# The causal mask added by VectorE's evictions, and the first mixture's results turned as 128 tokens and a stacked rest

## The chip, the cores and the metric

The kernel runs on one core of a Trainium2 chip. Five engines work side by side: TensorE (PE in the profile; its weight loads have a row of their own, PEld), VectorE (DVE), ScalarE (ACT), GpSimd (POOL) and SyncE (SP), which issues most DMAs. The metric is the device time of one execution in microseconds. Three runs before the change gave 395.3, 395.41 and 395.61 us, median 395.41 us.

## The reference: what is computed

```
# attention: B=2, H=8, S=576, D=64
scores = q @ k^T / 8
cum    = cumsum(max(s, 0))
scores = where(key later than query, -1e9, scores + min(-(cum_q - cum_k), 0))
x      = softmax(scores) @ v                       -> 1152 tokens of 512 numbers
# first mixture: 8 experts, at most `capacity` tokens each
e      = argmax(x @ w_gate);   g = softmax(x @ w_gate)[e]
x      = g * (max(x @ w1[e], 0) @ w2[e])           (0 for tokens beyond the capacity)
# second mixture: 8 experts, no capacity, own weights and a bias per modality
e      = argmax(x @ w_gate + bias[modality]);  g = softmax(...)[e]
out    = g * (max(x @ w1[e], 0) @ w2[e])
```

## The kernel before the change

**Attention** (up to about 96 us) goes over 8 pairs of heads, 16 heads (`for n in range(17)`, from line 612). A head's 576 queries are five tiles (`ROWS`, `QS`): 64 and four times 128. Their scores stand in four PSUM banks (`BANKS`): tiles 2 and 1 in the first, 3 and 0 in the second, tile 4 in two halves. `scores` (L474) fills a bank by two products (`qa`,`ka` and `qb`,`kb`; the second carries the rest of the precision and the sums of s). Where a bank reaches the diagonal, a third matmul adds the mask: the identity in bf16 (`identb`) is the weights, and `later`, 0 or -8e9, is what goes through. Then VectorE evicts every tile of the bank in one instruction (L510): scores times -0.125 into `sc`, and their running minimum into `nmx`. ScalarE takes the exponential with its sum (L515). One head later TensorE turns the exponentials block by block (`turned`, `pt`), VectorE and ScalarE copy them to `eT`, and `values` multiplies by v (`pa`, `pb`) once a pair; `close_pair` turns the results to tokens (`px`). GpSimd prepares the operands of the next pair (L370, L371, L377). All matmuls of attention stand in the order in which `pe` (L426) writes them; the other engines' order is set by a scheduler.

**First mixture** (111 to 264 us): eight slots of up to 192 tokens, one per expert, 160, 192, 136, 152, 132, 160, 144 and 168 wide (`WID`). TensorE's order is written by hand (`pin`): `mul` issues the products of the slot, and `step` moves a clock on, by which the generator `tail1` of the slot before is resumed between them. `tail1` computes the second mixture's logits from `yT` (features by tokens), then `back(k, yr, 0)` and `back(k, yr, 1)` turn the results to tokens: first 96 tokens, then the rest, four matmuls against the identity each (`pty`, L993), one for each 128 features. ScalarE evicts them times the gate into `yr` (L994). One DMA (L1067) writes `yr`, 2 x 96 rows of 520 numbers (512 results, gate, token, logits' bias), to `y1` in DRAM. The second mixture gathers its tokens from `y1` (L830).

**Second mixture** (264 us to the end): five slots, of which `tail2` also uses `back`.

Weights come by SP as pieces of 512 KB (`fetch`, L144 and L146), 7 of 8 ahead, into 8 buffers; SP issues its DMAs in order and waits at each.

Of the kernel before, what the change touches and what calls it, by code (L numbers as in the profile page):

```python
# [23 lines left out]
H1, H2, W1, W2, C1, C2 = HC[1], HC[2], W[1], W[2], C[1], C[2]  # L24
# [3 lines left out]
RW2 = 520  # L28
GATE, TOK, BIAS = 512, 513, 520
# [8 lines left out]
NOV = 7  # L38
# [54 lines left out]
def build(tc, ctx, spots, tab, qk, v, s, wg, wa, cap, mod, wg2, mb, wb, out):  # L93
    nc = tc.nc
    P = 128
# [5 lines left out]
    y1 = dram.tile([NCH * C1, RW2], F32, name="y1")  # L101
# [7 lines left out]
    ident = const.tile([P, P], F32, name="ident")  # L109
    ctab = const.tile([P, tab.shape[1]], F32, name="ctab")  # L110
    con = {}
    for name, (c0, shape) in spots.items():
        if len(shape) == 1:
            con[name] = ctab[:, c0:c0 + shape[0]]
        else:
# [11 lines left out]
                                 op0=ALU.add, op1=ALU.add)  # L127
# [11 lines left out]
    def fetch(src, e, i, pin=False):  # L139

        st = wst.tile([P, PIECE], F32, name="st")
        c0 = i * PIECE
        if isinstance(e, int):
            ins = nc.sync.dma_start(st, src[e, :, c0:c0 + PIECE])  # L144
        else:
            ins = nc.sync.dma_start(st, src[bass.ds(e, 1), :, c0:c0 + PIECE].rearrange("o p c -> (o p) c"))  # L146
        if pin:
            tc.keep_in_program_order(ins)
        return st

    first, xcs, written = [], [], []

    def awake(ps, a, b, n):

# [72 lines left out]
    with ExitStack() as actx:  # L227
        ap = actx.enter_context(tc.tile_pool(name="ap", bufs=2))
        ae = actx.enter_context(tc.tile_pool(name="ae", bufs=1))
# [19 lines left out]
        with tc.issue_after(pads.ins):  # L249
            summed = summed()  # L250
        make_identity(nc, ident)
        identb = ae.tile([P, P], BF16, name="identb")
        nc.gpsimd.tensor_copy(identb, ident)
        later = ae.tile([P, P + 64], BF16, name="later")
        nc.gpsimd.memset(later, 0.0)
        for c0, c1 in ((0, P), (P, P + 64)):
            nc.gpsimd.affine_select(out=later[:, c0:c1], in_=later[:, c0:c1], pattern=[[-1, c1 - c0]],
                                    compare_op=ALU.is_ge, fill=-8.0e9, base=0, channel_multiplier=1)
        ebuf = {}
        for t in range(1, NT):  # L260
            for j in range(2):
# [162 lines left out]
        def pe(op, *args, **kw):  # L424
            with tc.issue_after(order[-1]) if order else ExitStack():
                ins = op(*args, **kw)  # L426
            order[:] = [ins.ins]
            return ins
# [7 lines left out]
        def open_pair(p):  # L436
            pr_ = Part()
            pr_.p, pr_.b, pr_.hp, pr_.eTs = p, p // 4, p % 4, []
            pr_.qa, pr_.ka, pr_.qb, pr_.kb, pr_.vt = loads.pop(p)
            pairs.append(pr_)  # L440
            if p < 7:
                loads[p + 1] = load(p + 1)
            if p > 3:
                for i in range(2):
                    first.append(fetch(wa, 0, 2 * (p - 4) + i, pin=True))
            if p == 3:
                for i in range(2):
                    xc = const.tile([H1, 2, RW], F32, name=f"xc{i}")
                    with tc.issue_after(operands[-1]):
                        nc.gpsimd.memset(xc, 0.0)  # L450
                    xcs.append(xc)
                zrow = ac.tile([P, 1, DM], F32, name="zrow")
                with tc.issue_after(operands[-1]):
                    nc.gpsimd.memset(zrow, 0.0)
                tc.keep_in_program_order(nc.sync.dma_start(
                    out.rearrange("(p t) d -> p t d", t=9), zrow.to_broadcast([P, 9, DM])))

# [16 lines left out]
        def scores(h, bank, parts=(0, 1)):  # L474


            k, i = h.k, h.i
            qa, ka, qb, kb = k.qa[:, i], k.ka[:, i], k.qb[:, i], k.kb[:, i]
            if 0 in parts:
                h.ps[bank] = pss.tile([P, 512], F32, name="ps")  # L480
            ps = h.ps[bank]
            for t, o0, c0, c1 in bank:
                r, q0 = ROWS[t], QS[t]
                o = ps[:r, o0:o0 + c1 - c0]
                if 0 in parts:
                    pe(nc.tensor.matmul, o, qa[:, q0:q0 + r], ka[:, c0:c1], start=not o0, stop=False,
                       skip_group_check=True)
                if 1 in parts:
                    pe(nc.tensor.matmul, o, qb[:, q0:q0 + r], kb[:, c0:c1], start=False, stop=c1 <= q0,
                       skip_group_check=True)  # L490
            if 1 not in parts:
                return
            del h.ps[bank]
            t, o0, c0, c1 = bank[0]
            if t == 2:
                masked = ps[:, P:512].rearrange("p (u c) -> p u c", u=2)[:, :, 64:192]
                mask = later[:, 0:P].unsqueeze(1).to_broadcast([P, 2, P])
            elif t == 3:
                masked, mask = ps[:, 320:512], later
            else:  # L500
                masked, mask = ps[:, QS[4] - c0:c1 - c0], later[:, 0:P]
            if c1 > QS[t]:
                pe(nc.tensor.matmul, masked, identb, mask, start=False, stop=True, skip_group_check=True)
            for t, o0, c0, c1 in bank[::-1]:
                r, w = ROWS[t], QS[t] + ROWS[t]
                if c0 == 0:
                    h.sc[t] = ap.tile([P, S], F32, name="sc", bufs=3)
                low = h.nmx[t][:r] if c0 else 3.0e38
                h.nmx[t] = ap.tile([P, 1], F32, name="nmx", bufs=6)
                least[:] = [nc.vector.tensor_scalar(h.sc[t][:r, c0:c1], ps[:r, o0:o0 + c1 - c0], -0.125, low, op0=ALU.mult,  # L510
                                                    op1=ALU.min, accum_out=h.nmx[t][:r]).ins]
                if c1 == w:
                    n = 2 * k.hp + i
                    to = ebuf[t, i][:, :w] if t else ebuf[1, i][0:64, P:P + 64]
                    recent[:] = [nc.scalar.activation(to, h.sc[t][:r, :w], AF.Exp, bias=h.nmx[t][:r],  # L515
                                                      scale=-1.0, accum_out=rsum[:r, k.b, t, n:n + 1]).ins]

        moved, least = [], []
# [93 lines left out]
        for n in range(2 * 2 * 4 + 1):  # L612
# [24 lines left out]
            if n == 1:  # L637
                fills = tc.issue_after(filled.ins)
                fills.__enter__()
                for bb in range(B):  # L640
# [10 lines left out]
                                        fill=0.0, base=0, channel_multiplier=-1)  # L651
# [183 lines left out]
    def pin(ins):  # L835

        tc.keep_in_program_order(ins)
# [151 lines left out]
    def back(k, yr, i):  # L989
        r0, r = k.rows[i]  # L990
        pt = pt_.tile([r, DM], F32, tag="t", name="pty")
        for dt in range(DM // P):
            pin(nc.tensor.transpose(pt[:, dt * P:(dt + 1) * P], k.yT[:, dt, r0:r0 + r], ident))  # L993
        nc.scalar.mul(yr[:r, i, 0:DM], pt, k.xc[:r, i, GATE:GATE + 1])  # L994

    def absent(k):
        inv = mp.tile([HP, W[k.m]], F32, tag="inv", name="inv")
        nc.vector.tensor_scalar(inv, k.idx, float(OFF[k.m]), NONE, op0=ALU.is_ge, op1=ALU.mult)
        return inv

    def tail1(k, c):

        k.yr, l8 = yrs[c % 2], l8s[c % 2]
        nc.gpsimd.tensor_copy(k.yr[:, :, TOK], k.xc[:, :, TOK])
        yield k.T[0]
        p8 = pq.tile([P, k.c], F32, tag="q", name="p8")
        for kt in range(4):
            pin(nc.tensor.matmul(p8[32 * kt:32 * kt + 32], wg2s[:, kt, :], k.yT[:, kt, :], start=True, stop=True,
                   tile_position=(0, 32 * kt)))
        nc.vector.tensor_copy(l8[:, 0:k.c], p8)  # L1010
        back(k, k.yr, 0)
        yield k.T[1]
        pl = pq.tile([H1, 2, P], F32, tag="q", name="pl")
        for i in range(2):
            pin(nc.tensor.transpose(pl[:, i, :], l8[:, i * H1:(i + 1) * H1], ident))
        yield k.T[2]
        back(k, k.yr, 1)
        bc = [H1, 2, E]
        lg = mp.tile(bc, F32, name="lg2")
        nc.vector.tensor_reduce(lg, pl.rearrange("p i (k e) -> p i e k", k=4)[:, :, 0:E, :], axis=AX.X, op=ALU.add)  # L1020
# [41 lines left out]
        g = mp.tile([H1, 2], F32, name="g2")  # L1062
        nc.vector.tensor_reduce(g, ex, axis=AX.X, op=ALU.add)
        nc.vector.tensor_scalar_add(g, g, 1.0e-9)
        nc.vector.reciprocal(k.yr[:, :, GATE], g)

        nc.sync.dma_start(y1[c * C1:(c + 1) * C1, :].rearrange("(i p) w -> p i w", i=2), k.yr)  # L1067
        yield k.T[6] if k.early else k.T[4]
        for i in range(2):
            pin(nc.tensor.matmul(pl2, pos[:, i, :], colm[:, i, :], start=(c == 0 and i == 0), stop=True,  # L1070
# [195 lines left out]
    def clear(x):  # L1266
        tc.keep_in_program_order(nc.gpsimd.memset(x, 0.0))

    yrs = [sm.tile([H1, W1, RW2], F32, name=f"yr{i}") for i in range(2)]
    l8s = [sm.tile([P, C1], F32, name=f"l8{i}") for i in range(2)]  # L1270
    at(0, 2, lambda: clear(xcs[2]))
    for lst in (lists, list2):
# [148 lines left out]
    with tc.If(more_ > 0):  # L1421
        latest.clear()
        nc.sync.dma_start(y1[E * C1:, :].rearrange("(p t) d -> p t d", p=H1),
                          yrs[0][:, 0:1, :].to_broadcast([H1, NOV * W1, RW2]))
        tot1 = nc.values_load(reso[0:1, 0, NOV:NOV + 1], min_val=0, max_val=NOV)
        with tc.If(tot1 > 0):
            latest.clear()
            again()
            beyond()
            nested(1, tot1, reso, list1b, 0, NOV, wa, lambda k, i: tail1(k, E + i))  # L1430
            listed(list2[:H2], pl2, 2)
            left()
            latest.clear()
        tot2 = nc.values_load(info["res"][0:1, 0, NSLOT2:NSLOT2 + 1], min_val=0, max_val=NSLOT2)
        nested(2, tot2, info["res"], list2, 0, NSLOT2, wb, lambda k, i: tail2(k))
        latest.clear()
# [47 lines left out]
```

## Time and profile before

| what | value |
|---|---|
| median of three runs | 395.41 us |
| the profiled execution | 396.09 us |
| its span in the profile | 394.0 us (2.1 us lie around it) |
| TensorE busy | 380.8 us, 97% of the span |
| VectorE, ScalarE, GpSimd busy | 196.7, 178.9, 130.0 us |
| granted TensorE clock, mean | 0.996 |
| chain that ended last, share of TensorE | 82% |

How to read it: busy times are averages over stages with different limits, so the stages are read one by one. Matmuls overlap, and a row's duration is longer than the step to the next row; what one costs in a row of matmuls is the difference of two starts. The chain of waits is followed back from the last instruction and shows which engine the end hung on at each time.

### The profile page before, as it was taken

To read this page: it belongs to the slowest core of one execution; us is meant where nothing else is said; L and a number is where in the kernel's file an instruction comes from. 1 tells how busy PE (TensorE), PEld (TensorE's weight loads), DVE (VectorE), ACT (ScalarE), POOL (GpSimd) and SP (SyncE) were. 2 spreads that over 40 slices of the span, in tenths; PEclk is the share of its full clock that TensorE was granted. 3 is DMA by queue.
4 is the path that set the end of the run, shared out by engine and by line. 5 is a ranking of instruction groups with operands and counts; after the bars stand their busy time and mean duration, and the time that the engine had idled before them with its cause. 6 is when DMAs were issued, how large, how long until landed. Compare 5 with 4: busy or idle time off the path is not lost.

```text
span 394.0 us, 8765 instructions
## 1 busy us (share of the span) xinstructions
PE 380.8 (97%) x3128; PEld 355.6 (90%) x3128; DVE 196.7 (50%) x785; ACT 178.9 (45%) x473; POOL 130.0 (33%) x180
## 2 busy tenths in 40 slices
PE   6799999999999999999999999999999999999993
PEld 3688888898689999999999999999999999999992
DVE  6977779987826773341515061559822335211110
ACT  6999999987315642121212121255423464131130
POOL 4776877660164221330202003000335256010020
PEclk9999999999999999999999999999999999999998
DMA  5865699802159962978798779871279356010010
GB/s 186 289 192 157 235 378 364 284 3 79 51 142 303 352 222 62 321 230 294 221 326 262 241 238 278 262 246 56 59 255 342 107 166 208 26 38 21 2 54 24
DMA packets 26882, 74.63 MB, mean 189 GB/s; under 512 B 5527, under 2 KB 7959, under 8 KB 26828
## 3 DMA queue, kind: packets, MB, share of 16 engines
q1 hardware_dynamic: 24120, 66.73, 50.6%
q0 software_dynamic: 2624, 7.19, 6.5%
q8 instruction: 27, 0.44, 0.5%
q14 instruction: 27, 0.22, 0.2%
q10 hardware_dynamic: 84, 0.04, 0.0%
HBM read 63.97 MB, written 10.62 MB: 189 GB/s over the span
## 4 chain that ended last, share of the span: by engine, by line
PE 82%; issue 7%; DMA 4%; DVE 3%; POOL 2%; POOLq 0%; SPq 0%; ACT 0%; DVEq 0%; ACTq 0%
PE ps L907 30%; PE ps L915 7%; PE ps L916 7%; PE ps L917 7%; PE ps L426 6%; PE pt L426 6%; PE pb L426 4%; PE ps L911 3%; PE pty L993 3%; PE pa L426 2%; PE ptx L871 2%; PE px L426 2%; DMA out<-yo,oi 2%; PE ps L913 1%; DMA qkd<-in_qk 1%
## 5 line engine op out<-in xcount | busy, mean ns | idle before, releaser
L907 PE MATMUL ps<-xn,st 128*128 128x160 f32 (+6 forms) x512 | 70.4, 290 | 0.3 <-ACT xn L892 0.3
L907 PEld LDWEIGHTS ps<-xn,st 128*128 128x128 f32 x512 | 66.2, 190 | 0.5 <-ACT xn L892 0.4
L907 PE MATMUL ps<-hidden,st 128*128 128x160 f32 (+5 forms) x448 | 62.4, 293 | 0.0
L907 PEld LDWEIGHTS ps<-hidden,st 128*128 128x128 f32 x448 | 58.5, 190 | 0.0
L515 ACT ACTIVATE e<-sc,nmx 128x192 f32<-128x192 f32 (+4 forms) x80 | 44.8, 561 | 2.2 <-DVE sc L510 2.1
L973 DVE COPY yT<-ps 128x276 f32<-128x276 f32 (+6 forms) x22 | 8.0, 362 | 69.6 <-ACT yT L972 69.6
L915 PE MATMUL ps<-xs,hi 128*128 128x276 f32 x128 | 38.5, 300 | 0.0
L915 PE MATMUL ps<-hidden,hi 128*128 128x276 f32 x128 | 38.1, 298 | 0.0
L917 PE MATMUL ps<-xs,lo 128*128 128x276 f32 x128 | 37.2, 290 | 0.0
L916 PE MATMUL ps<-xs,hi 128*128 128x276 f32 x128 | 37.1, 290 | 0.0
L917 PE MATMUL ps<-hidden,lo 128*128 128x276 f32 x128 | 37.1, 290 | 0.0
L916 PE MATMUL ps<-hidden,hi 128*128 128x276 f32 x128 | 37.1, 290 | 0.0
L830 POOL DMA_INDIRECT xc<-x,idx x14 | 14.9, 1064 | 60.1 <-DVE eq L1030 44.2
L972 ACT COPY yT<-ps 128x276 f32<-128x276 f32 (+6 forms) x22 | 7.1, 322 | 60.6 <-PE ps L907 33.2
L426 PE MATMUL pt<-ident,e 128*128 128x128 f32 x224 | 33.0, 275 | 0.8 <-ACT eT L537 0.7
L510 DVE TENSOR_SCALAR_CACHE_REDUCE sc<-ps 128x192 f32<-128x192 f32 (+4 forms) x80 | 31.2, 418 | 1.6 <-PE ps L426 0.3
L426 PE MATMUL ps<-ka,qa 128*128 128x320 f32 (+2 forms) x96 | 29.9, 327 | 1.9 <-DVE qa L390 1.3
L1077 POOL DMA_INDIRECT out<-yo,oi x13 | 12.4, 953 | 54.5 <-ACT yo L994 44.9
L805 DVE TENSOR_TENSOR lo<-st,hi 128x512 fp32r<-128x512 f32 x40 | 28.8, 759 | 1.5 <-ACT hi L803 1.4
L803 ACT CAST hi<-st 128x512 fp32r<-128x512 f32 x48 | 27.4, 619 | 0.0
L426 PEld LDWEIGHTS pt<-ident,e 128*128 128x128 f32 x224 | 24.4, 140 | 1.8 <-ACT eT L537 0.9
L426 PE MATMUL ps<-kb,qb 128*128 128x320 f32 (+2 forms) x96 | 24.3, 298 | 1.6 <-POOL kb L377 0.8
(313 smaller groups left out, 839.1 us busy)
## 6 DMA issues: line engine op xcount, KB each, us to landing
st<-in_wa SPq DMA_DIRECT2D x64, 512.0 KB, 5.4
st<-in_wb SPq DMA_DIRECT2D x24, 512.0 KB, 4.6
qkd<-in_qk SPq DMA_DIRECT2D x6, 1152.0 KB, 5.5
y<-yr SPq DMA_DIRECT2D x8, 390.0 KB, 4.3
vt<-in_v SPq DMA_DIRECT2D x8, 320.0 KB
qkd<-in_qk SPq DMA_DIRECT2D x4, 576.0 KB, 5.3
out<-zrow SPq DMA_DIRECT2D x1, 2304.0 KB
x<-xrow SPq DMA_DIRECT2D x2, 768.0 KB
```

The source lines that it names most:

```text
L426: ins = op(*args, **kw)
L510: least[:] = [nc.vector.tensor_scalar(h.sc[t][:r, c0:c1], ps[:r, o0:o0 + c1 - c0], -0.125, low, op0=ALU.mult, op1=ALU.min, accum_out=h.nmx ...
L515: recent[:] = [nc.scalar.activation(to, h.sc[t][:r, :w], AF.Exp, bias=h.nmx[t][:r], scale=-1.0, accum_out=rsum[:r, k.b, t, n:n + 1]).ins]
L803: nc.scalar.copy(hi[:, c:c + h], st[:, c:c + h])
L805: eng.tensor_tensor(lo[:, c:c + h], st[:, c:c + h], hi[:, c:c + h].bitcast(F32), op=ALU.subtract)
L830: nc.gpsimd.indirect_dma_start(out=k.xc[:r, i, 0:rw], out_offset=None, in_=src, in_offset=bass.IndirectOffsetOnAxis(ap=idx[:r, i:i + 1], a ...
L907: pin(nc.tensor.matmul(out[:, 0:c], w[:, o:o + P], mv, start=first, stop=last, skip_group_check=True))
L911: pin(nc.tensor.matmul(out[:, 0:2 * c], hi, mv.rearrange("p s c -> p (s c)"), start=first, stop=False, skip_group_check=True))
L915: pin(nc.tensor.matmul(out[:, 0:c], hi, mv[:, 0, :], start=first, stop=False, skip_group_check=True))
L916: pin(nc.tensor.matmul(out[:, 0:c], hi, mv[:, 1, :], start=False, stop=False, skip_group_check=True))
L917: pin(nc.tensor.matmul(out[:, 0:c], lo, mv[:, 0, :], start=False, stop=last, skip_group_check=True))
L1077: put = nc.gpsimd.indirect_dma_start(out=out, out_offset=bass.IndirectOffsetOnAxis(ap=oi[:, i:i + 1], axis=0), in_=yr[:, i, :], in_offset= ...
```

## The change

Two edits in one.

**Mask.** The third matmul of a bank is gone, and `identb` with it. `later` is now 128 x 576 in fp32: 448 columns of 0 and a triangle of -8e9 in the last 128. An eviction that reaches the diagonal is a `tensor_tensor_reduce`, (scores + a slice of `later`) times -0.125 with the running minimum; the slice is as long as the eviction and ends at the diagonal. The first half of tile 4 keeps the old instruction.

**Turning.** `rows1` takes the place of `back` in `tail1`. The first 128 tokens are turned by four matmuls. The rest (32, 64, 8, 24, 4, 32, 16 and 40 tokens in the eight slots) is first copied by VectorE to `rest`, and 4 blocks of 128 features, or 2 where 4 don't fit in 128 columns, are turned as one matmul, stacked on the partitions. ScalarE copies without the gate. The results go to `y1` by one DMA for the 128 tokens and one for each stacked block; `yr` holds only the last 8 columns, with the product of both gates, and has a DMA of its own. Rows of `y1` that no slot writes are set to 0 by one DMA during attention.

```diff
-        identb = ae.tile([P, P], BF16, name="identb")
-        nc.gpsimd.tensor_copy(identb, ident)
-        later = ae.tile([P, P + 64], BF16, name="later")
+        later = ae.tile([P, S], F32, name="later")
         nc.gpsimd.memset(later, 0.0)
-        for c0, c1 in ((0, P), (P, P + 64)):
-            nc.gpsimd.affine_select(out=later[:, c0:c1], in_=later[:, c0:c1], pattern=[[-1, c1 - c0]],
-                                    compare_op=ALU.is_ge, fill=-8.0e9, base=0, channel_multiplier=1)
+        nc.gpsimd.affine_select(out=later[:, S - P:S], in_=later[:, S - P:S], pattern=[[-1, P]],
+                                compare_op=ALU.is_ge, fill=-8.0e9, base=0, channel_multiplier=1)
...
+            if p == 6:
+                tc.keep_in_program_order(nc.sync.dma_start(
+                    y1[0:E * C1].rearrange("(c r) w -> r c w", c=E)[P:C1, :, 0:DM],
+                    zrows[0][0:C1 - P].to_broadcast([C1 - P, E, DM])))
...
-            t, o0, c0, c1 = bank[0]
-            if t == 2:
-                masked = ps[:, P:512].rearrange("p (u c) -> p u c", u=2)[:, :, 64:192]
-                mask = later[:, 0:P].unsqueeze(1).to_broadcast([P, 2, P])
...
-            if c1 > QS[t]:
-                pe(nc.tensor.matmul, masked, identb, mask, start=False, stop=True, skip_group_check=True)
...
-                least[:] = [nc.vector.tensor_scalar(h.sc[t][:r, c0:c1], ps[:r, o0:o0 + c1 - c0], -0.125, low, op0=ALU.mult,
-                                                    op1=ALU.min, accum_out=h.nmx[t][:r]).ins]
+                if c1 == w:
+                    m0 = S - P - (QS[t] - c0)
+                    least[:] = [nc.vector.tensor_tensor_reduce(h.sc[t][:r, c0:c1], ps[:r, o0:o0 + c1 - c0],
+                                                               later[:r, m0:m0 + c1 - c0], -0.125, low, op0=ALU.add,
+                                                               op1=ALU.min, accum_out=h.nmx[t][:r]).ins]
...
+    def rows1(k, c, b):
+        r0, r, g = (P, k.c - P, 4 if 4 * (k.c - P) <= P else 2) if b else (0, P, 1)
+        to = yts[c % 2][b][:g * r, 0:DM // P // g]
+        pt = pt_.tile([g * r, DM // P // g, P], F32, tag="t", name="pty")
+        for u in range(DM // P // g):
+            pin(nc.tensor.transpose(pt[:, u, :], k.rest[:, g * u:g * u + g].rearrange("p g r -> p (g r)") if b else
+                                    k.yT[:, u, 0:P], ident))
+        nc.scalar.copy(to, pt)
+        rows = y1[c * C1 + r0:c * C1 + r0 + r, 0:DM].rearrange("r (u g d) -> r u g d", g=g, d=P)
+        for i in range(g):
+            nc.sync.dma_start(rows[:, :, i, :], to[r * i:r * i + r])
...
         nc.vector.tensor_copy(l8[:, 0:k.c], p8)
-        back(k, k.yr, 0)
+        k.rest = mp.tile([P, 4, k.c - P], F32, name="rest")
+        nc.vector.tensor_copy(k.rest, k.yT[:, :, P:])
+        rows1(k, c, 0)
...
-        back(k, k.yr, 1)
+        rows1(k, c, 1)
...
-        nc.vector.reciprocal(k.yr[:, :, GATE], g)
-        nc.sync.dma_start(y1[c * C1:(c + 1) * C1, :].rearrange("(i p) w -> p i w", i=2), k.yr)
+        nc.vector.reciprocal(g, g)
+        nc.vector.tensor_tensor(k.yr[:, :, GATE - DM], g, k.xc[:, :, GATE], op=ALU.mult)
+        nc.sync.dma_start(y1[c * C1:(c + 1) * C1, DM:RW2].rearrange("(i p) w -> p i w", i=2), k.yr)
```

How the instructions now stand. VectorE at the start of attention, before (`qa`, `kb` are operands of the first pair's second head, `sc` the evicted scores, `nmx` their minimum):

```order
L390 TENSOR_TENSOR kb_122<-qkd,ka 64x576
L390 TENSOR_TENSOR qa<-qkd,qb_121 64x576
L510 TENSOR_SCALAR sc,nmx<-ps 128x192
L510 TENSOR_SCALAR sc,nmx<-ps 128x320
L510 TENSOR_SCALAR sc,nmx<-ps 64x64
L390 TENSOR_TENSOR kb_122<-qkd,ka 64x576
```

and now:

```order
L387 TENSOR_TENSOR kb_122<-qkd,ka 64x576
L504 ISA sc,nmx<-ps,later 128x192
L504 ISA nmx 128x1
L387 TENSOR_TENSOR qa<-qkd,qb_121 64x576
L504 ISA sc,nmx<-ps,later 128x320
L504 ISA nmx 128x1
L504 ISA sc,nmx<-ps,later 64x64
L504 ISA nmx 64x1
L387 TENSOR_TENSOR kb_122<-qkd,ka 64x576
```

The first eviction moved ahead of `qa`. An eviction is two rows, the second of which writes the minimum; before, the trace shows such a second instruction too, where this listing shows one row. Later in attention VectorE keeps its order but for small steps such as the reciprocal of the sums. SP in the third slot's tail, before (`st` weights, `y_64` is `y1`):

```order
L146 DMA st<-in_wa 128x1024
L1067 DMA y_64<-yr_2026 96x2x520
L146 ISA
L146 DMA st<-in_wa 128x1024
L146 ISA
```

and now:

```order
L146 DMA st<-in_wa 128x1024
L1006 DMA y_64<-yt_1976 128x512
L1006 DMA y_64<-yt_1977 8x128 x4
L146 ISA
L146 DMA st<-in_wa 128x1024
L1082 DMA y_64<-yr_1974 96x2x8
L146 ISA
```

The results' DMAs stand one weight piece ahead of the small one that took the old one's place. On TensorE nothing moves but the instructions that go (48 mask matmuls with 48 weight loads, and 22 of the 64 `pty` matmuls of the eight tails).

## Rows read from the trace of the kernel before

**Rows 1.** The page, parts 1 and 4: busy time, share; chain by engine
```profile
span 394.0 us, 8765 instructions
...
PE 380.8 (97%) x3128; PEld 355.6 (90%) x3128; DVE 196.7 (50%) x785; ACT 178.9 (45%) x473; POOL 130.0 (33%) x180
...
PE 82%; issue 7%; DMA 4%; DVE 3%; POOL 2%; POOLq 0%; SPq 0%; ACT 0%; DVEq 0%; ACTq 0%
```

**Rows 2.** Chain of waits around attention: start, us, work it hung on
```profile
12.40 0.68 POOL qb L370
...
20.97 0.74 PE ps L426 x4
21.71 1.13 PE pa L426 x12
...
87.57 1.13 PE pa L426 x12
```

**Rows 3.** Busy time by stage; length, then PE, PEld, DVE, ACT, POOL, clock, DMA
```profile
21.71:87.57 65.86, 65.86 (x608) 58.16 (x609) 53.94 (x242) 60.81 (x188) 48.14 (x56) 1.00 0.67 236
...
111.37:264.25 152.88, 152.88 (x1261) 149.75 (x1261) 63.38 (x272) 44.12 (x113) 31.37 (x45) 1.00 0.79 253
```

**Rows 4.** Busy time in one pair of heads, same columns
```profile
43.61:54.55 10.94, 10.94 (x102) 9.66 (x104) 8.77 (x40) 10.14 (x32) 9.05 (x14) 1.00 1.02 388
```

**Rows 5.** Timeline of PE, one head: start, duration, line, operation
```profile
50.92 0.28 PE L426 MATMUL ps<-later,identb 128*128 128x256 bf16 x1
51.04 0.71 PE L426 MATMUL pt<-ident,e 128*128 128x128 f32 x5
...
52.02 0.22 PE L426 MATMUL ps<-kb,qb 128*64 128x64 f32 x1
52.08 0.26 PE L426 MATMUL ps<-later,identb 128*128 128x192 bf16 x1
52.18 0.60 PE L426 MATMUL pt<-ident,e 128*128 128x128 f32 x4
...
53.15 0.23 PE L426 MATMUL ps<-later,identb 128*128 128x128 bf16 x1
53.22 0.71 PE L426 MATMUL pt<-ident,e 128*128 128x128 f32 x5
```

**Rows 6.** Timeline of VectorE, start of attention
```profile
9.52 0.76 DVE L390 TENSOR_TENSOR qa<-qkd,qb 64x576 fp32r<-64x576 f32 x1 [1.15 <-ACT qa L390]
10.31 0.36 DVE L510 TENSOR_SCALAR_CACHE_REDUCE sc<-ps 128x192 f32<-128x192 f32 x1
...
11.25 0.76 DVE L390 TENSOR_TENSOR kb<-qkd,ka 64x576 fp32r<-64x576 f32 x1
```

**Rows 7.** Timeline of PE there: the last products of the first scores
```profile
9.34 0.47 PE L426 MATMUL ps<-kb,qb 128*128 128x320 f32 x2 [0.41 <-DMA kb<-s_sb]
```

**Rows 8.** Groups of VectorE instructions by form: count, busy us, mean ns, idle before
```profile
L805 DVE TENSOR_TENSOR lo<-st,hi 128x512 fp32r<-128x512 f32 x40 | 28.8, 759 | 1.5 <-ACT hi L803 1.4
...
L510 DVE TENSOR_SCALAR_CACHE_REDUCE sc<-ps 128x448 f32<-128x448 f32 x16 | 9.8, 614 | 0.3 <-ACT e L515 0.2
...
L510 DVE TENSOR_SCALAR_CACHE_REDUCE sc<-ps 128x320 f32<-128x320 f32 x16 | 7.7, 484 | 0.0
...
L510 DVE DVE_READ_ACCUMULATOR sc<-ps 128x1 f32 x64 | 5.2, 81 | 0.0
...
L583 DVE TENSOR_TENSOR xrow<-px,rinv 128x384 f32<-128x384 f32 x7 | 3.8, 546 | 0.0
...
L126 DVE TENSOR_TENSOR_SCAN cum<-s_sb,zero 16x576 f32<-16x576 f32 x1 | 1.3, 1281 | 0.0
```

**Rows 9.** Instructions on one tile: a custom VectorE instruction, min, median, max ns
```profile
L1343 DVE CUSTOM_DVE_ANT_0 both<-s2res,s1res x1: 136/136/136, 284.0 to 284.0; 1x2 uint16<-1x2 uint16 x1
```

**Rows 10.** Timeline of PE, fourth slot of the first mixture: the second turning
```profile
172.46 0.60 PE L993 MATMUL pty<-ident,yT 128*40 128x128 f32 x4
172.90 2.75 PE L907 MATMUL ps<-xn,st 128*128 128x152 f32 x20
```

**Rows 11.** Timeline of SP in the fourth slot
```profile
175.05 0.33 SPq L1067 DMA_DIRECT2D y<-yr  x1
```

**Rows 12.** SP's waits for TensorE to free weight buffers: us, times, longest
```profile
SPq L146 <- PE ps L907: 75.1, 40, 10.9
```

More of the change, by code (lines that the diff above doesn't have):

```diff
@@ L149, in fetch @@
         return st
-    first, xcs, written = [], [], []
+    first, xcs, written, zrows = [], [], [], []
     def awake(ps, a, b, n):
@@ L454, in open_pair @@
                     nc.gpsimd.memset(zrow, 0.0)
+                zrows.append(zrow)
                 tc.keep_in_program_order(nc.sync.dma_start(
@@ L488, in scores @@
                 if 1 in parts:
-                    pe(nc.tensor.matmul, o, qb[:, q0:q0 + r], kb[:, c0:c1], start=False, stop=c1 <= q0,
+                    pe(nc.tensor.matmul, o, qb[:, q0:q0 + r], kb[:, c0:c1], start=False, stop=True,
                        skip_group_check=True)
@@ L493, in scores @@
             del h.ps[bank]
-            t, o0, c0, c1 = bank[0]
-            if t == 2:
-                masked = ps[:, P:512].rearrange("p (u c) -> p u c", u=2)[:, :, 64:192]
-                mask = later[:, 0:P].unsqueeze(1).to_broadcast([P, 2, P])
[L498 to L501, printed above, removed]
-            if c1 > QS[t]:
-                pe(nc.tensor.matmul, masked, identb, mask, start=False, stop=True, skip_group_check=True)
             for t, o0, c0, c1 in bank[::-1]:
@@ L509, in scores @@
                 h.nmx[t] = ap.tile([P, 1], F32, name="nmx", bufs=6)
-                least[:] = [nc.vector.tensor_scalar(h.sc[t][:r, c0:c1], ps[:r, o0:o0 + c1 - c0], -0.125, low, op0=ALU.mult,
-                                                    op1=ALU.min, accum_out=h.nmx[t][:r]).ins]
+                if c1 == w:
[3 more added lines that the diff above has]
+                                                               op1=ALU.min, accum_out=h.nmx[t][:r]).ins]
+                else:
+                    least[:] = [nc.vector.tensor_scalar(h.sc[t][:r, c0:c1], ps[:r, o0:o0 + c1 - c0], -0.125, low,
+                                                        op0=ALU.mult, op1=ALU.min, accum_out=h.nmx[t][:r]).ins]
                 if c1 == w:
@@ L1003, in tail1 @@
         k.yr, l8 = yrs[c % 2], l8s[c % 2]
-        nc.gpsimd.tensor_copy(k.yr[:, :, TOK], k.xc[:, :, TOK])
+        nc.gpsimd.tensor_copy(k.yr[:, :, TOK - DM], k.xc[:, :, TOK])
         yield k.T[0]
@@ L1267, in clear @@
         tc.keep_in_program_order(nc.gpsimd.memset(x, 0.0))
-    yrs = [sm.tile([H1, W1, RW2], F32, name=f"yr{i}") for i in range(2)]
+    yrs = [sm.tile([H1, W1, RW2 - DM], F32, name=f"yr{i}") for i in range(2)]
+    yts = [[sm.tile([P, n, P], F32, name=f"yt{i}{n}") for n in (4, 2)] for i in range(2)]
     l8s = [sm.tile([P, C1], F32, name=f"l8{i}") for i in range(2)]
@@ L1423, in build @@
         nc.sync.dma_start(y1[E * C1:, :].rearrange("(p t) d -> p t d", p=H1),
-                          yrs[0][:, 0:1, :].to_broadcast([H1, NOV * W1, RW2]))
+                          rings[2][0][:, 0:1, :].to_broadcast([H1, NOV * W1, RW2]))
         tot1 = nc.values_load(reso[0:1, 0, NOV:NOV + 1], min_val=0, max_val=NOV)
```

## The prediction

> **What bounds the kernel now.** I read the page's shares first: TensorE is busy 97% of the span and holds 82% of the chain that ended last, VectorE 3%, GpSimd 2% [rows 1]. The reader should see that only work taken off TensorE, or a new wait put onto it, can move the end. The chain itself says where that holds [rows 2]: from 12.40 to 20.97 us it hangs on GpSimd, which makes the operands of the first pairs, and from 20.97 on it alternates between TensorE's scores (ps) and values (pa), once a pair, to 87.57. So the first three heads run at GpSimd's pace, the thirteen heads behind them at TensorE's. The stages agree [rows 3]: between 21.71 and 87.57 TensorE is busy all 65.86 us, ScalarE 60.81, VectorE 53.94; in the first mixture TensorE is busy all 152.88 us and VectorE only 63.38. A single pair lasts 10.94 us and TensorE works all of it, ScalarE 10.14, GpSimd 9.05, VectorE 8.77 [rows 4]. TensorE has no gap to fill, so an instruction removed there brings the end nearer until the next engine is full, and the next one is ScalarE, only 0.80 us behind.
>
> **The change part by part: the mask matmuls.** Each head loses three. Their durations (0.28, 0.26, 0.23) overlap what follows, so I take steps from start to start [rows 5]: 50.92 to 51.04 is 0.12, 52.08 to 52.18 is 0.10, 53.15 to 53.22 is 0.07, in all 0.29. Not all of that comes back. The transposes that follow take steps of about 0.11 (five in a row end 0.71 after the start, four 0.60), and the product ahead of the second mask is only 64 rows long and steps on after 0.06 (52.02 to 52.08); the transposes' weights must then load behind it, which the mask matmul hid. I take 0.11 for the first, 0.06 for the second and 0.07 for the third: 0.24 us a head, and keep 0.29 as the other end. Thirteen heads on TensorE's pace give 13 x 0.24 = 3.12 (up to 3.77); the first three give nothing, since GpSimd sets their pace [rows 2].
>
> **The start.** VectorE now evicts the first 192 columns ahead of qa. Before, qa began at 9.52, the eviction followed at 10.31 and kb at 11.25 [rows 6]. The eviction needs the products that begin at 9.34 and last 0.47 [rows 7]: it can begin at 9.87 at the earliest and holds VectorE for some 0.28 beside its read, so qa begins at about 10.15 to 10.2, and kb, after the other two evictions as before, at about 11.55 instead of 11.25. GpSimd's chain from 12.40 moves by the same 0.3. That is a loss of 0.3; its ends are 0 (GpSimd had its own operands to make and did not need that kb) and 0.65 (the whole wait of qa). Attention in all: -3.12 + 0.3 = -2.8.
>
> **The evictions.** Five of a head's six get a second input of fp32 from SBUF. The cover is what VectorE has free in a pair, at the pace the removal would set: 10.94 - 2 x 0.24 = 10.46, less 8.77, is 1.69 us for ten evictions, 0.17 each. The trace of before has no such instruction; it bounds it so [rows 8]. With one input, 320 columns take 484 ns and 448 take 614: 1.02 ns a column, and 549 for 384 between them. An ordinary two-input instruction from PSUM and SBUF takes 546 for the same 384: no difference, the lower end. The upper end is a two-input instruction with both inputs in SBUF, 759 for 512, where one input would take 614 + 64 x 1.02 = 679: 0.08 more each. The new instruction is a custom one; the only such row, on one column, lasts 136 ns [rows 9], less than the 157 that remain of an eviction without its columns (484 - 320 x 1.02), so nothing says its start is dearer. The separate read of the minimum, 81 ns, stood behind each eviction already [rows 8]. I take 0, since L583 is nearest: it reads the same memories. Even 0.08 leaves VectorE at 9.6 of 10.46, hidden.
>
> What VectorE has left is less than what matters on ScalarE: its 10.14 of 10.46 leaves 0.32 a pair. It kept up with 0.80 spare; I forecast that it also does with 0.32, and if not, a rival below prices it. GpSimd loses a copy and gets a longer memset ahead of the start, where it is not pushed; its 9.05 fits in 10.46.
>
> **The turning.** The second turning of a slot takes four matmuls from 172.46 to the next product at 172.90, 0.44, so 0.11 each [rows 10]. Six slots do with one, two (of 64 and 40 tokens left over) with two: 6 x 3 + 2 x 2 = 22 matmuls go, 22 x 0.11 = 2.42. The upper end is 0.12 each, by the step in attention [rows 5], 2.64. The first turning keeps four matmuls; the identity's 128 columns go through either way, and 128 rows of weights instead of 96 are what attention's transposes have, which also step on after 0.11 [rows 5]. In this stage nothing else is near a limit [rows 3], VectorE's copy to rest (128 to 256 columns a partition, 0.29 to 0.42 by the prices above) and the small product of gates lie within its 89 us of idle time, and the copy stands two steps of the order ahead of the turning that needs it. ScalarE's copy without a gate is not dearer than the multiplication.
>
> **The DMAs.** SP issues one large result DMA in 0.33 us [rows 11]; now each tail issues one for 128 tokens, two or four for the stacked blocks and the small one: up to five more, 1.65 us of SP a tail, behind which weight pieces queue. SP waits 75.1 us for TensorE to free weight buffers, in 40 waits [rows 12], nearly 2 us each, and pieces are 7 of 8 ahead: hidden. If that cover went, up to 8 x 1.65 would show, but pieces would have to run out first. Two weight pieces move behind the 1 MB of zeros at pair 6; at the 236 GB/s of that stage 1 MB takes 4.4 us [rows 3], and the first expert starts only at 111.37, some 20 us later: nothing.
>
> **Sum**: -3.12 + 0.3 - 2.42 = -5.24. The profiled execution took 396.09, so 390.85; the median 395.41 lies 0.68 below that execution, and on it the forecast is 390.2.
>
> **The rivals.**
>
> *One half stays out.* Either ScalarE cannot give up more of its idle time: it then sets 10.94 a pair and the mask brings nothing, -2.42 + 0.3 = -2.1, 393.3. For it: 93% busy with waits on every head [rows 4]; against: nothing in the chain hangs on it between 20.97 and 87.57 [rows 2]. Or the second turning, now behind a copy on another engine, waits some 0.33 a slot, as much as it saves, and the change does not do there what it says: -2.8, 392.6. Against that one: the two steps between. Together 0.22.
>
> *The new eviction runs at half rate: slower.* A custom instruction that carries a running minimum may need two passes a column. The trace has one instruction with a carried value: the scan over 576 columns takes 1281 ns, where one pass would be 157 + 588 = 745 [rows 8]. At that rate a head gets 192 + 320 + 64 + 448 + 288 = 1312 columns more, 1.34 us; a pair on VectorE 8.77 + 2.68 = 11.45, which is over TensorE's 10.94. The loss is at least 0.51 a pair; if VectorE, like ScalarE now, gets no more than 93% busy, 12.3 and 1.36 a pair. Over 6.5 pairs that is 3.3 to 8.8, middle 6.1; one head's 1.34 at the start, less 2.42 from the turnings: +5.0, 400.4. It decides from 0.17 us more per eviction (VectorE becomes the pace), and the whole turns slower from about 0.25 (10.94 + 0.32 a pair eats the 2.1 of the tails). For it: the scan; against: the eviction of before carries a minimum too and runs at one pass (614 for 448). [...] Chance 0.10.
>
> **How the numbers follow.** Forecast 0.65: its own range is 389.0 (0.29 a head, no loss at the start, 0.12 a turning: 3.77 + 2.64 = 6.4) to 391.4 (0.65 at the start gives 390.5, and pairs of 10.60 instead of 10.46 add 0.14 x 6.5 = 0.9). One half out 0.22, slower 0.10, and 0.03 for no change. A measurement of this kernel can tell 0.2%, 0.8 us, from no change; the first two cases are both faster, so 0.86 faster with a little taken off for the blends between them and the third, 0.03 same, 0.11 slower. The range takes in the forecast and the one-half cases, 388.7 to 393.4, and leaves out the slow one.
>
> **What the profile after would show.** Pairs that start 10.46 apart instead of 10.94 in the chain of waits; no matmul of later; the first pa at about 22.0 instead of 21.71; the 448-column eviction at about 614 ns, ScalarE idle 0.3 a pair, TensorE still without a gap; 42 pty matmuls instead of 64 and a second turning of one step, 0.11. The forecast is wrong if VectorE's evictions appear in the chain (over 780 ns for 448 columns), if ScalarE's exponentials do, or if SP's waits shrink to nothing while TensorE waits for weights.

## The result, and the profile after

The changed kernel took 390.83 us in the median of four runs (390.53 to 391.5), the kernel before 395.36 beside it: ratio 0.9888, interval 0.9873 to 0.9903, 4.5 us faster. That lies 0.6 above the forecast of 390.2 and within the range.

The page of the changed kernel, parts 1 and 4, answering to [rows 1]:

```profile
span 389.1 us, 8687 instructions
...
PE 376.5 (97%) x3058; PEld 353.6 (91%) x3058; DVE 198.6 (51%) x801; ACT 175.9 (45%) x473; POOL 126.8 (33%) x178
...
PE 77%; issue 7%; DMA 6%; DVE 3%; POOL 3%; ACT 1%; SPq 1%; POOLq 1%; DVEq 0%; ACTq 0%
```

TensorE has 4.3 us less to do, is still 97% busy and still leads the chain. The second pa of the kernel before, for the step of a pair, then the chain of waits of the changed kernel, for [rows 2]:

```profile
32.66 1.13 PE pa L426 x12
```

```profile
12.03 1.01 PE ps L423 x3
...
21.54 1.13 PE pa L423 x12
...
32.02 1.13 PE pa L423 x12
...
43.66 0.65 POOL qb L367
...
52.06 0.68 POOL qb L367
...
52.76 9.98 DMA qkd<-in_qk
...
66.58 0.99 ACT e L513 x4
67.94 0.66 PE pt L423 x4
...
74.72 1.13 PE pa L423 x12
...
85.19 1.13 PE pa L423 x12
...
108.90 13.31 PE ps L905 x96
```

Two things are to be seen. Pairs now start 10.48 apart (21.54, 32.02), where it was 10.95 (21.71, 32.66). And between 43.66 and 67.94 the chain leaves TensorE: it goes over GpSimd's operands, whose end (52.74) lets the next load be issued, then over that load (from 52.76) and then over ScalarE, which it did nowhere in this stretch before. Busy time by stage and by pair (columns as in [rows 3, 4]):

```profile
21.54:85.19 63.65, 63.28 (x571) 56.51 (x573) 54.38 (x244) 60.57 (x188) 48.15 (x56) 1.00 0.74 261
...
42.42:52.90 10.48, 10.48 (x96) 9.39 (x95) 8.81 (x39) 10.11 (x32) 9.16 (x12) 1.00 1.00 365
...
63.44:74.65 11.21, 10.84 (x101) 9.57 (x100) 10.12 (x50) 10.60 (x36) 8.45 (x13) 1.00 0.93 308
74.65:85.12 10.47, 10.47 (x95) 9.37 (x94) 9.37 (x44) 9.97 (x32) 7.04 (x6) 1.00 0.49 191
```

The six pairs from the first pa to the seventh take 63.65 us where they took 65.86 [rows 3]: 2.21 less, not the forecast 6 x 0.48 = 2.88. The pair from 63.44, called the seventh below since it prepares the operands of the seventh pair of heads, is the exception; TensorE stands still there for 0.37. VectorE and ScalarE carry the routing of the first batch in that pair (its tokens' logits, maximum, exponential, rank). The same pair of the kernel before:

```profile
65.43:76.55 11.12, 11.12 (x106) 9.82 (x106) 9.98 (x49) 10.34 (x34) 7.64 (x8) 1.00 0.90 327
```

It took 0.17 more than its neighbours, all of it TensorE's own work. Less 0.48 it should have come to 10.64; it came to 11.21.

The evictions, by form (columns as in [rows 8]):

```profile
L504 DVE CUSTOM_DVE_ANT_0 sc<-ps,later 128x448 f32<-128x448 f32 x16 | 9.8, 611 | 0.0
...
L504 DVE CUSTOM_DVE_ANT_0 sc<-ps,later 128x320 f32<-128x320 f32 x16 | 7.8, 485 | 0.3 <-ACT e L513 0.2
...
L504 DVE DVE_READ_ACCUMULATOR2_ANT nmx<- 128x1 f32 x64 | 5.1, 80 | 0.0
```

611, 485 and 80 ns stand against 614, 484 and 81 [rows 8]: the second input costs nothing that shows in the time, and the half-rate rival is dead. (Those of 192 columns take 350 ns in the mean against 332; with the mask added twice, below, they take 331.)

The second turning of the fourth slot on TensorE is one step of 0.11 where it was 0.44 [rows 10]:

```profile
169.48 0.27 PE L1001 MATMUL pty<-ident,rest 128*32 128x128 f32 x1
169.59 1.59 PE L905 MATMUL ps<-xn,st 128*128 128x152 f32 x11
```

From the first expert to the first turning of the second mixture (108.90 to 289.61, by the chain; the second row is the kernel before, whose stretch began at 111.37 [rows 3]) it is 180.71 against 183.15: 2.44 less. TensorE is busy for 180.67 and 183.11 of it.

```profile
289.61 0.44 PE pty L991 x4
```

```profile
294.52 0.44 PE pty L993 x4
```

At the start, VectorE of the changed kernel, then TensorE, for [rows 6, 7]:

```profile
5.12 0.46 DVE L387 CAST qb<-qkd 64x576 fp32r<-64x576 f32 x1 [0.28 <-DMA qkd<-in_qk]
...
9.39 0.36 DVE L504 CUSTOM_DVE_ANT_0 sc<-ps,later 128x192 f32<-128x192 f32 x1 [1.57 <-PE ps L423]
...
9.78 0.76 DVE L387 TENSOR_TENSOR qa<-qkd,qb 64x576 fp32r<-64x576 f32 x1
...
11.22 0.76 DVE L387 TENSOR_TENSOR kb<-qkd,ka 64x576 fp32r<-64x576 f32 x1
```

```profile
11.20 0.61 PE L423 MATMUL ps<-ka,qa 128*128 128x320 f32 x1 [1.36 <-DVE nmx L504]
```

Read against the arrival of the first operands (the cast to qb, at 5.12; before at 5.67), kb starts 6.10 later, where it was 11.25 - 5.67 = 5.58: 0.52 lost. That arrival differs between executions (the cast started between 4.89 and 5.67 in the traces of this study). The two profiled executions lie 5.25 apart, more than the medians' 4.53; 0.55 of that is the one before getting its operands later.

### The profile page after: what moved, and what is told of

Its sections match the earlier page's. It is cut to its first block, busy times and chain, and to the rows that moved or that the text cites. A ratio compares the mean times of both kernels' runs of the same rounds, so it can differ in the third digit from the quotient of the medians.

```text
span 389.1 us, 8687 instructions
## 1 busy us (share of the span) xinstructions
PE 376.5 (97%) x3058; PEld 353.6 (91%) x3058; DVE 198.6 (51%) x801; ACT 175.9 (45%) x473; POOL 126.8 (33%) x178
## 4 chain that ended last, share of the span: by engine, by line
PE 77%; issue 7%; DMA 6%; DVE 3%; POOL 3%; ACT 1%; SPq 1%; POOLq 1%; DVEq 0%; ACTq 0%
PE ps L905 30%; PE ps L913 7%; PE ps L914 7%; PE ps L915 7%; PE pt L423 5%; PE ps L423 4%; DMA qkd<-in_qk 4%; PE ps L909 3%; PE pb L423 2%; PE ptx L869 2%; PE pa L423 2%; DMA out<-yo,oi 2%; PE px L423 2%; PE pty L1001 1%; PE ps L911 1%
## 5 line engine op out<-in xcount | busy, mean ns | idle before, releaser
L423 PE MATMUL pt<-ident,e 128*128 128x128 f32 x224 | 35.1, 288 | 0.5 <-ACT xu L552 0.4
L423 PE MATMUL ps<-ka,qa 128*128 128x320 f32 (+2 forms) x96 | 31.0, 337 | 2.6 <-DVE nmx L504 1.4
L423 PEld LDWEIGHTS pt<-ident,e 128*128 128x128 f32 x224 | 25.9, 146 | 1.5 <-ACT xu L552 0.5
L828 POOL DMA_INDIRECT xc<-x,idx x14 | 13.9, 995 | 40.8 <-PE pr L1055 23.4
L984 DVE SCALAR_TENSOR_TENSOR hidden<-ps,hidden 128x552 fp32r<-128x552 f32 x16 | 11.7, 732 | 28.3 <-ACT hidden L982 28.2
L504 DVE CUSTOM_DVE_ANT_0 sc<-ps,later 128x192 f32<-128x192 f32 (+1 forms) x64 | 24.5, 413 | 2.7 <-PE ps L423 1.6
```

Source lines behind the costliest of these rows:

```text
L504: least[:] = [nc.vector.tensor_tensor_reduce(h.sc[t][:r, c0:c1], ps[:r, o0:o0 + c1 - c0], later[:r, m0:m0 + c1 - c0], -0.125, low, op0=ALU ...
L828: nc.gpsimd.indirect_dma_start(out=k.xc[:r, i, 0:rw], out_offset=None, in_=src, in_offset=bass.IndirectOffsetOnAxis(ap=idx[:r, i:i + 1], a ...
L984: fence(relu, nc.vector.scalar_tensor_tensor(k.hs[:, 2 * j:2 * j + 2, 1, :], k.b, 0.0, hi.bitcast(F32), op0=ALU.max, op1=ALU.subtract))
```

## The experiments

**The halves apart.** First the mask alone (the diff's turning parts taken back), then the turning alone (its mask parts taken back).

> The mask half alone; turnings, result DMAs and zeros as before. My theory: the two halves lie in different stages and add up, and the turnings gave the 2.4 us of 22 matmuls, so the mask gave the rest of 4.5: 393.3 us (392.8 to 393.7). Its pairs start 10.47 apart except one; VectorE's first kb comes about 0.5 us late against the first load, and the granted clock falls to 0.5 between 11 and 18 us as in the changed kernel. Rival, the removed matmuls pay in full (13 heads x 0.24) and the start costs nothing: 392.3. Rival, the mask brings nothing and the turnings all: 395.3.

> The turning half alone, with its result DMAs and the 1 MB of zeros; mask as before. My theory: 22 matmuls x 0.11 = 2.42, so 393.0 us (392.7 to 393.3); attention as before, pairs 10.94 apart, the clock at 1.00 in all of the start; the 152.88 us of the first mixture become 150.4. Rival, the zeros or the smaller DMAs cost weight pieces time and the mask half gave more than it seems: 393.8 or more. Rival, the stacked turning waits for its copy: 395.

The mask alone took 393.27 us (ratio 0.9951, 0.9938 to 0.9964), the turning alone 392.92 (0.9944, 0.9931 to 0.9957), the kernel before 395.45. So 2.2 and 2.5 us, together 4.7: they add up, within the intervals, to the 4.5 of both. Which half sits in which stage shows in the traces: with the mask alone the seventh pair takes 11.19, with the turning alone pairs take 10.94 as before. The granted clock fell to 0.50 with the mask alone, though only between 13 and 17 us, and stayed at 1.00 with the turning alone.

**The mask's price on VectorE.** The kernel before with the mask added twice, by its matmuls and by the new evictions.

```diff
-                least[:] = [nc.vector.tensor_scalar(h.sc[t][:r, c0:c1], ps[:r, o0:o0 + c1 - c0], -0.125, low, op0=ALU.mult,
-                                                    op1=ALU.min, accum_out=h.nmx[t][:r]).ins]
+                if c1 == w:
...
+                    least[:] = [nc.vector.tensor_tensor_reduce(h.sc[t][:r, c0:c1], ps[:r, o0:o0 + c1 - c0],
+                                                               late2[:r, m0:m0 + c1 - c0], -0.125, low, op0=ALU.add,
...
```

> The kernel before, with its mask matmuls, whose evictions add the mask a second time by the new instruction (masked scores get it twice); VectorE keeps the order of before. My theory: the new instruction costs what the old one did (it lies beside TensorE's work, and its mean is within 0.01 of the old one's), so 395.4 us (395.1 to 395.7), and what the mask half gave is all from the matmuls. Rival, it is dearer by up to 0.08 each, still hidden: 395.4 to 395.9. Rival, it takes two passes: 398 or more.

395.2 us, ratio 0.9996 (0.9987 to 1.0005): no difference. The 448 columns take 608 ns there. So the evictions are neither a cost nor a gain, and what the mask half gave is the matmuls'.

**The turning's price on TensorE.** The changed kernel with the rest turned by four matmuls again.

```diff
-        r0, r, g = (P, k.c - P, 4 if 4 * (k.c - P) <= P else 2) if b else (0, P, 1)
+        r0, r, g = (P, k.c - P, 1) if b else (0, P, 1)
...
-    yts = [[sm.tile([P, n, P], F32, name=f"yt{i}{n}") for n in (4, 2)] for i in range(2)]
+    small = sm.tile([P, 4, P], F32, name="small")
+    yts = [[sm.tile([P, 4, P], F32, name=f"yt{i}"), small] for i in range(2)]
```

> The changed kernel with the second turning by four matmuls again, from the copied rest, and one result DMA for it; everything else as changed. My theory: the whole gain of the first mixture is the 22 matmuls at 0.11, so 390.83 + 2.42 = 393.25 us (393.0 to 393.6). Rival, part of it came from ScalarE's copy without a gate or from the first turning with 128 rows: 392.0 or less. Rival, the copies and small DMAs had cost something too: above 393.6.

393.14 us, ratio 0.9944 (0.9931 to 0.9958): 2.3 of the 2.4 are back. In the fourth slot the four take 0.44 again:

```profile
169.87 0.60 PE L1001 MATMUL pty<-ident,rest 128*8 128x128 f32 x4
170.31 1.97 PE L905 MATMUL ps<-xn,st 128*128 128x152 f32 x14
```

So the 22 matmuls are the gain; VectorE's copies and the first turning's 128 rows, which this run keeps, neither add nor take: it stands where the mask alone does (393.27). The DMAs went back with the matmuls, from two or four for the rest to one, so their price is not tested by itself; that 2.3 came back where 22 matmuls at 0.11 are 2.42 leaves little for it.

**The start.** One more condition: the first eviction behind qa.

```diff
+            second.append(vec[-2])
...
+                    with behind_all([second.pop()] if second else []):
+                        least[:] = [nc.vector.tensor_tensor_reduce(h.sc[t][:r, c0:c1], ps[:r, o0:o0 + c1 - c0],
```

> The changed kernel with one more condition: the very first eviction follows qa of the second head on VectorE, the order that the kernel before had. My theory: kb comes 0.5 us earlier against the first load, GpSimd's chain with it, and TensorE's clock does not fall at 11 us; 390.4 us (390.1 to 390.6), 0.4 under the changed kernel. Rival, kb's delay is hidden since TensorE and ScalarE set the pace of the first heads: 390.8, no difference that five rounds tell. Rival, the low clock is what costs: 7 us at half clock cost up to 2 us of TensorE, so 389.3.

390.58 us, ratio 0.9877 (0.9862 to 0.9891). The interval overlaps that of the changed kernel, so the time alone does not show it. The trace does; VectorE:

```profile
5.25 0.46 DVE L387 CAST qb<-qkd 64x576 fp32r<-64x576 f32 x1 [0.42 <-DMA qkd<-in_qk]
...
10.84 0.76 DVE L387 TENSOR_TENSOR kb<-qkd,ka 64x576 fp32r<-64x576 f32 x1
```

kb starts 5.59 after the operands' cast, as before (5.58). By TensorE's timeline (which has pa 0.07 ahead of the chain) the first pa starts 21.10 - 5.25 = 15.85 after the cast, against 21.47 - 5.12 = 16.35 in the changed kernel: half a microsecond came back. The other runs repeat it: in the four that have the changed evictions but the first one behind qa, the first pa starts 15.83 to 16.04 after the cast, in the seven with the eviction ahead of qa 16.35 to 16.47. The clock fell all the same, for a shorter time (half as long, 3.4 us); that part of my theory was wrong, and the last section shows that the length is not the order's doing.

**The seventh pair.** I first took the late load for the cause.

```diff
             if p == 3:
...
-                tc.keep_in_program_order(nc.sync.dma_start(
-                    out.rearrange("(p t) d -> p t d", t=9), zrow.to_broadcast([P, 9, DM])))
+            if p == 7:
+                tc.keep_in_program_order(nc.sync.dma_start(
+                    out.rearrange("(p t) d -> p t d", t=9), zrows[0].to_broadcast([P, 9, DM])))
```

> The changed kernel with the 2304 KB DMA of zeros to the output issued in the last pair of attention instead of the fourth. My theory: in the changed kernel the operands of the seventh pair, issued at 52.76, landed at 62.8 and held ScalarE and GpSimd up, so that one pair took 11.21 instead of 10.48; without the zeros ahead of them they land in time and the pair takes 10.6 or less: 390.2 us (389.9 to 390.5). Rival, ScalarE itself is the pace of that pair (it also turns logits there) and the late load only the last to come: 390.8. Rival, the zeros collide with the results of attention at its end: 391.2.

391.34 us, ratio 0.9897 (0.9883 to 0.9911): a miss. The load was in time, and the pair took 11.59, more than the changed kernel's 11.21. ScalarE of the changed kernel, then of this one:

```profile
62.83 0.68 ACT L365 CAST qa<-qkd 128x576 fp32r<-128x576 f32 x1 [0.39 <-DMA qkd<-in_qk]
```

```profile
65.21 0.24 ACT L300 ACTIVATE ex<-d 128x40 f32<-128x40 f32 x1 [0.43 <-DVE d L279]
65.65 0.78 ACT L514 ACTIVATE e<-sc,nmx 128x576 f32<-128x576 f32 x1 [0.20 <-DVE nmx L505]
```

The wait for the load is gone, and in its place ScalarE waits for VectorE, which is late with a step of the routing, `d`, the logits less their maximum. So my theory became: two late arrivals, and each alone is enough. It passed over why `d` is late. VectorE's `d` and GpSimd's product at that time, in the changed kernel:

```profile
64.02 0.29 DVE L279 TENSOR_TENSOR d<-lsum,mx 128x40 f32<-128x40 f32 x1
64.33 1.41 POOL L368 TENSOR_TENSOR qa<-qkd,qb 64x576 fp32r<-64x576 f32 x1
```

and in this run:

```profile
64.15 1.02 DVE L279 TENSOR_TENSOR d<-lsum,mx 128x40 f32<-128x40 f32 x1
63.71 1.41 POOL L368 TENSOR_TENSOR qa<-qkd,qb 64x576 fp32r<-64x576 f32 x1
```

The same small instruction takes 1.02 instead of 0.29 and ends 0.05 after GpSimd's qa. The late load had held GpSimd up, so that its qa began after `d`; with the load in time it begins before. The 0.73 that `d` lost is most of the 0.77 by which this pair is longer than 10.82, what the changed kernel's takes without its wait of 0.39 for the load. That `d` waits for GpSimd is read from these times; no run moved GpSimd's product to test it.

Next, the routing one pair later: first from the one-hot on (this diff), then all of it (one more condition, ahead of the maximum), then all of it with the zeros late too.

```diff
-            if k.p == 5:
+            if k.p == 6:
                 with tc.issue_after(k.least):
                     postponed.pop()()
...
-            if p == 4:
+            if p == 5:
...
                 route(0, k.least)
```

> The changed kernel with the routing of the first batch (its logits' maximum, one-hot, exponential, rank) issued one pair later, in the eighth pair instead of the seventh. My theory now: the pair of 11.21 us is long since VectorE (10.12) and ScalarE (10.60) carry that routing beside their usual work, and TensorE then waits 0.37 for them; moved, the seventh pair takes 10.5 and the eighth, in which no operands are made for a next pair, takes it for 0.2 at most: 390.4 us (390.1 to 390.6). Rival, the eighth pair is held up as much: 390.8. Rival, the late rank delays the lists at the end of attention: 391.3 or more.

> The changed kernel with all of the first batch's routing one pair later (the run before moved it from the one-hot on and left its maximum and exponential in the seventh pair). My theory now: the seventh pair has two late arrivals, either enough: its operands from DRAM (ScalarE waits for them at 62.83) and the logits' difference that the exponential on ScalarE needs. This takes away the second alone, so the pair stays near 10.9, held by the operands: 390.6 us (390.4 to 390.8). Rival, the routing alone held it: 10.5 for the pair, 390.2.

> As the run before, and the DMA of zeros to the output in the last pair. My theory: with both late arrivals gone the seventh pair takes 10.5 like its neighbours, the eighth 10.7 with the routing's matmuls: 0.5 us below the changed kernel, 390.3 us (390.0 to 390.5). Rival, ScalarE itself is full there (10.6 of 11.2): the pair stays at 10.9 or more, 390.7.

390.73 us (ratio 0.9884, 0.9869 to 0.9899), 391.51 (0.9892, 0.9876 to 0.9909) and 391.42 (0.9893, 0.9876 to 0.9909; the kernel before took 395.76 beside these last two). All three miss, and none is faster than the change. But the pairs show the mechanism. In the first the seventh pair takes 10.88. With all of the routing gone and the load late (the second of the three), then with both gone (the third):

```profile
63.40:74.14 10.74, 10.64 (x95) 9.43 (x94) 8.93 (x39) 10.35 (x34) 8.34 (x12) 1.00 0.96 338
74.14:85.50 11.36, 11.04 (x100) 9.63 (x99) 11.09 (x50) 10.40 (x33) 6.93 (x6) 1.00 0.32 99
```

```profile
63.59:74.15 10.56, 10.56 (x95) 9.43 (x95) 8.85 (x39) 10.14 (x32) 7.79 (x10) 1.00 0.81 276
74.15:85.48 11.33, 11.02 (x100) 9.61 (x99) 11.06 (x50) 10.40 (x33) 6.90 (x6) 1.00 0.40 121
```

Without either the seventh pair takes 10.56, TensorE without a gap; with the late load alone 10.74. So either adds, but they are not alike. What the load costs is what ScalarE waits for it: the four kernels with routing and load as in the change (it, the mask alone, the four turnings, the start) wait 0.31 to 0.39, their pairs take 11.13 to 11.21, and pair less wait is 10.82 in each. But the eighth pair, which now holds the routing, takes 11.33 with VectorE busy for 11.06 of them; that it would take the routing for 0.2 is wrong. Here too one small instruction is long, `ge` on 5 columns, which takes 0.17 in the changed kernel; in the third run, beside GpSimd's kb:

```profile
76.96 1.42 DVE L289 TENSOR_SCALAR ge<-mn 128x5 f32<-128x5 f32 x1
76.85 1.49 POOL L375 TENSOR_TENSOR kb<-qkd,ka 64x576 fp32r<-64x576 f32 x1 [1.59 <-ACT ka L373]
```

It ends 0.04 after kb. Where the eighth pair has the routing from the one-hot on and `ge` runs ahead of kb in 0.16 (the first of the three runs), the pair takes 10.68.

> The changed kernel with both: the first eviction behind qa, and the routing of the first batch one pair later. My theory: the two gains add up: -0.25 to -0.5 at the start and -0.4 at the seventh pair, 390.0 us (389.7 to 390.3). Rival, the routing moved gives nothing: 390.5.

> As the run before, and the first eviction behind qa as in the kernel before. My theory: the start's 0.3 comes on top: 390.0 us (389.7 to 390.2), the fastest of all. Rival, as above without the pair: 390.4.

> The changed kernel with the first eviction behind qa, the zeros to the output in the last pair, and the routing moved from the one-hot on only (maximum, difference and exponential stay in the seventh pair). My theory: VectorE is the pace of whichever pair holds the whole routing (11.33 for the eighth when all was moved there), so a split between two pairs, with the operands in time, leaves both near 10.6: 390.0 us (389.8 to 390.3), the fastest. Rival, the exponential's wait for VectorE, 0.43 when the zeros alone were moved, stays and the seventh pair takes 11 again: 390.5.

390.46 us (ratio 0.9882, 0.9867 to 0.9897), 390.97 (0.9878, 0.9862 to 0.9895) and 390.68 (0.9880, 0.9864 to 0.9897). All three miss their ranges. In the last the exponential's wait stays (0.42) and the seventh pair takes 11.35, the rival's case; `d` takes 1.01 there and ends with GpSimd's qa again (64.47, 64.42). My theory took VectorE to be full with the routing, but of its 11.06 us in the eighth pair above 1.25 were `ge` beside GpSimd. In the first the seventh pair takes 11.12 where the same routing took 10.88 above: ScalarE waits 0.51 for the load instead of 0.27, and pair less wait is 10.61 in both. All carry a gain at the start (0.31 to 0.52 by the first pa), and no interval leaves that of the change: a version that beats it is not shown.

## Why the prediction was right, and where it was 0.6 off

- **The mask matmuls, 0.24 a head**: right. 10.95 to 10.48 a pair is 0.47. That the second mask matmul gives back less than its step, because the transposes' weights come up behind a short product, fits: the weight loads of the four transposes behind it now begin 0.01 ahead of them (29.77, 29.78) where they began 0.09 ahead (52.09, 52.18), the four now take 0.49 in the chain where they took 0.44, and the full 0.58 a pair did not come.
- **Evictions at no cost**: right, 611 against 614, and the doubled mask gave no difference. From 320 to 448 columns the new instruction takes (611 - 485) / 128 = 0.98 ns a column, the old one 1.02: no second pass, for which the scan (1281 ns for 576 columns) had spoken.
- **The start, 0.3**: right in kind; kb lost 0.52 and the first pa 16.35 - 15.97 = 0.38 against the operands (15.97 is 21.64 - 5.67, by the timeline). My sum was short twice: from qa at 10.15 to 10.2, the step from qa to kb less the eviction's 0.28 [rows 6] gives kb at 11.60 to 11.65, not 11.55; and the eviction held VectorE for 0.39 (9.39 to 9.78), not 0.28. And the chain of the changed kernel goes from 12.03 to the first pa over TensorE, not over GpSimd as I forecast; the last section says why.
- **Thirteen heads**: mis-sized, twice. "I forecast that it also does with 0.32" (ScalarE) held in five pairs of six. In the seventh it failed, by 0.57: the single pair of [rows 4], from which I took the slack, has no routing in it, and in the pair that has, VectorE and ScalarE had 9.98 and 10.34 to do already. This is the rival in which ScalarE becomes the pace, in one pair of six, and the sign that I had named for it is there: ScalarE's exponentials stand in the chain (66.58), in this pair alone. But only 0.18 of the 0.57 is that; 0.39 is ScalarE's wait for the load of operands, which my sum put at nothing. In the kernel before ScalarE came to it 10.30 after its issue (53.81 to 64.11) and did not wait; now it comes sooner, and the load takes 9.98. It was luck, not forecast, that the load was late enough to keep GpSimd's qa out of the way of `d`. The thirteenth head lies behind the seventh pa, where TensorE waits for others in turn: from 87.57 to the first expert it was 23.80 and is 23.71, 0.09 instead of 0.24.
- **The turnings, 2.42**: right, 2.44.
- **The DMAs hidden**: right. The five result DMAs of a tail take SP 3.56 us from first to last, of which 0.84 is a wait for ScalarE's copy; one issue takes 0.36 in the median of 36 (0.27 to 1.57), where I took 0.33 [rows 11]. The wait I had not priced. SP's waits for TensorE's buffers shrank from 75.1 us in 40 to 56.6 in 32, still 1.8 each: the cover held.

```profile
168.86 3.56 SPq L1006 DMA_DIRECT2D y<-yt  x5
```

```profile
L1006 SPq DMA_DIRECT2D y<-yt x36: 273/360/1566, 130.7 to 264.9; - x36
```

```profile
SPq L146 <- PE ps L905: 56.6, 32, 11.1
```

By these terms: -2.21 (six pairs), -0.09 (behind them), +0.38 (start), -2.44 (turnings) is -4.36, against 4.53 in the medians and 5.24 forecast. Of the 0.88 between the two sums the pairs are 0.67. The step that failed is the slack read from one pair and used for all: in the seventh pair it did not cover the routing (0.18) nor the load's arrival (0.39).

## What to carry to other kernels

A cover is read from the fullest period, not from a typical one: go through all the periods that an edit shortens and look for the one with extra work on the engine that is next. Count the arrival of loads as a cover too: it shrinks with the period (here ScalarE came 10.30 us after a load's issue and did not wait, and with the shorter pairs it came sooner and waited 0.39). When that period turns out long, take every late arrival away before naming one as the cause, and where a fix makes it longer still, look for an instruction that takes longer than it did elsewhere: removing one delay can move another engine's work on top of it (here `d`, 0.29 to 1.02 us). And a removed instruction that leaves an engine's order to a scheduler can move work at the start (here kb, by 0.52 us), so compare starts against the arrival of the first data.

## What the runs showed that I had not expected

TensorE's granted clock fell to 0.50 for some 6.8 us at the start of the changed kernel, after TensorE had stood idle for 1.36 us (9.84 to 11.20); in the kernel before it stayed at 1.00. Windows of the changed kernel (columns as in [rows 3]):

```profile
10.00:11.00 1.00, 0.00 (x0) 0.00 (x0) 0.99 (x4) 1.00 (x4) 0.00 (x0) 0.96 0.29 62
11.00:12.00 1.00, 0.61 (x1) 0.29 (x1) 0.94 (x5) 1.00 (x6) 0.00 (x0) 0.50 0.94 281
...
17.00:18.00 1.00, 1.00 (x7) 1.00 (x6) 0.86 (x4) 1.00 (x4) 0.91 (x7) 0.62 1.02 403
18.00:19.00 1.00, 1.00 (x10) 1.00 (x9) 0.91 (x5) 1.00 (x3) 0.95 (x1) 1.00 0.67 133
```

Five transposes in a row took 1.27 us there instead of 0.71. But neither the edit nor the idle time alone decides it. With the same idle time of 1.36 or 1.37 us the clock was low as long in one other run (its mean over the execution is 0.988 in both) and half as long in five (3.4 us with the mask alone and with the zeros late; means 0.992 to 0.994). With 0.6 us idle it stayed up in the kernel before (0.996) and with the turning alone (0.998), and fell, half as long, with the mask added twice (0.993). With the first eviction behind qa (0.8 us idle) it fell in two runs (0.993) and stayed up in two (0.995). What else decides it stays open.

It cost next to nothing that the traces show. The first pa starts 2.04 after the start of GpSimd's last kb both here (19.43, 21.47) and with the first eviction behind qa (19.06, 21.10); it is 2.04 to 2.06 in the nine traces without mask matmuls in which the clock was low half as long or not at all. The 6.8 us used up TensorE's slack: here it has no gap from 12.03 to the first pa and does not wait for that kb any more (with the first eviction behind qa it waits 0.46), and in the other run of 6.8 us the step is 2.15, so up to 0.1. Whether keeping TensorE busy in the gap at 9.84 would give anything was not tried by itself.
